# Short matmul tiles filled up with zeros to the full height: k and v in five chunks of 128 rows, the transform's row 288 in tiles of 97

## The chip, the core and the metric

One core of a Trainium2 chip runs the whole program in one launch. TensorE (PE, with its weight loads PEld) multiplies, VectorE (DVE), ScalarE (ACT) and GpSimd (POOL) work on tiles in the on-chip memory, and SyncE (SP) issues all DMA transfers of this kernel. The metric is the device time of one execution in microseconds (us), as the median of several runs; smaller is better.

## What is computed

Three layers follow each other on 8 batches, 8 heads, 576 rows and 64 channels (512 columns in all):

```python
def _attn_ref(q, k, v, g_norm):
    kv = np.einsum('bhsd,bhse->bhde', k, v)          # sums over the 576 rows
    out = np.einsum('bhsd,bhde->bhse', q, kv)
    rms = np.sqrt(np.mean(out * out, axis=-1, keepdims=True) + 1e-06)
    return out / rms * g_norm

def _moe_ref(x, w_ch1, w_ch2):
    mixed = np.real(fft(fft(x, axis=1), axis=2))     # over rows, then over columns
    u = x + mixed
    un = (u - mean(u)) / np.sqrt(var(u) + 1e-06)     # over the 512 columns
    return u + np.maximum(un @ w_ch1, 0.0) @ w_ch2   # 512 -> 2048 -> 512

def _moe2_ref(x, U, V, w_ch1, w_ch2):
    u = x + (x.T @ U @ V).T                          # over the rows, rank 32
    return u + np.maximum(u @ w_ch1, 0.0) @ w_ch2
```

## The kernel before

**Tiles and stages.** The two MLP layers run in 2 x 9 blocks of 512 rows (`BT`), each in 16 steps `n`: step `n` computes one 128-wide slice of the hidden layer (`emit_l1`, lines 168 to 170) and adds the slice before it to the outputs (`emit_l2`, lines 188 to 194). A factor is split into a high and a low part, so each product takes three matmuls with 512 moving columns.

**Attention and the transform beside the MLP.** Batch 0 goes ahead of the loop. Batches 1 to 7 are cut into pieces by `batch_tasks` and hung on fixed steps of blocks 0 to 6 through the table `side`. For batch b, `load_kv` (lines 400 to 406) brings k and v into a tile `kv` of 128 partitions: four chunks of 128 rows with two DMAs (line 404) and the last 64 rows of both with a third (line 405); for batch 0 this is done once for each half of the columns. `t_kv` (lines 237 to 249) multiplies k by v in two halves. A half has two groups of five matmuls, one for each chunk, of 128, 128, 128, 128 and 64 rows (`KT`, line 29). They are plain f32, and the trace shows each as two records of 128 columns, so a half has 20 records. `t_o` (line 262) multiplies q by the result; `t_norm` and the `t_fold_` functions prepare the transform on DVE, ACT and POOL.

**The transform over the rows.** By symmetry 289 of the 576 rows are left: 256 in two full tiles, 33 in a third. `seq_dft` (lines 336 to 347) adds up six full matmuls of 290 columns. For the cosine half (p = 0) there follows one of a single row, row 288 (line 345: `z288` from the table, `e288` from the data, both at partition 32), and then one of 97 rows that holds the remaining 32 rows three times (line 347; 96 rows for the sine half). `t_s1` calls it for two column halves and both p, `t_mu` once for the means. `e288` is made for each batch by ACT (line 321) and DVE (line 334); `z288` once, from the table `cz` (line 225). The transform over the columns is `t_s2` (lines 373 to 375).

**Order.** `manual_schedule` keeps every engine's instructions in the order in which the code issues them, and each engine's queue runs in that order. SP's queue carries all loads and stores, among them the MLP's weights in 64-bit form (`raw`, line 77, two buffers), which DVE, ACT and POOL turn into f32 (`w_conv` in block 0, `w_pre` in blocks 1 to 7). A weight load is issued when the conversion before it has read its buffer.

Of the kernel before, what the change touches and what calls it, by code (L numbers as in the profile page):

```python
# [10 lines left out]
F32 = mybir.dt.float32  # L11
F32R = mybir.dt.float32r
U32 = mybir.dt.uint32
AF = mybir.ActivationFunctionType
ALU = mybir.AluOpType
# [4 lines left out]
B, H, S, D = 8, 8, 576, 64  # L20
NH = S // 2 + 1
DM, DFF, RANK = 512, 2048, 32
# [3 lines left out]
NQ = 4 * C + 98  # L26
NS = 290
ND = 258
KT = (128, 128, 128, 128, 64)
BT = 512  # L30
NB = NT // BT
NF = DFF // 128
# [2 lines left out]


@with_exitstack
def kernel(ctx: ExitStack, tc: tile.TileContext, qT, kvm, kvt, gn, w1a, w2a, w1b, w2b,
                      ucat, v4, tabs, outT):
    nc = tc.nc  # L40
    f32 = lambda ap: ap.bitcast(F32)
# [12 lines left out]
    def side_bank(nm):  # L54
        if early:
            k = len(early) % 6
            early.append(True)
            if k < 4:
                return ps_acc.tile([128, 512], F32, tag=f"acc{k}", name=nm)
        return ps_s.tile([128, 512], F32, tag="side", name=nm)  # L60
# [7 lines left out]
    xe0 = com.tile([C, 3, B], F32, name="xe0")  # L68
# [130 lines left out]
    at = att_ctx.enter_context(tc.tile_pool(name="at", bufs=1))  # L199
# [3 lines left out]
    tb = {}  # L203
# [11 lines left out]
    def split_table(nm):  # L215

        t = tb.pop(nm)
        p, n = t.shape
        h = at.tile([p, n], F32R, name=nm + "h")
        nc.scalar.activation(out=h, in_=t, func=AF.Copy)  # L220
        if nm[1] == "z":
            nc.gpsimd.tensor_tensor(out=h[32:64], in0=t[32:64], in1=f32(h[32:64]), op=ALU.subtract)
            if nm == "cz":
                z = at.tile([33, n], F32R, name="z288")
                nc.scalar.activation(out=z[32:33], in_=t[96:97], func=AF.Copy)
                tb["z288"] = z[32:33]
            tb[nm] = h
            return
        l = at.tile([p, n], F32R, name=nm + "l")
        nc.gpsimd.tensor_tensor(out=l, in0=t, in1=f32(h), op=ALU.subtract)  # L230
        tb[nm + "h"], tb[nm + "l"] = (v.rearrange("p (k n) -> p k n", k=2) for v in (h, l))

    st = {}

    kvbd = com.tile([128, 4, 128], F32, name="kvbd")

    def t_kv(b, half):
        kv = st[b]["kv"]
        ps = side_bank(f"kv{b}_{half}")
        for j in range(2):  # L240
            cols = slice(256 * half + 128 * j, 256 * half + 128 * j + 128)
            for t in range(5):
                n = KT[t]
                nc.tensor.matmul(out=ps[:, 128 * j:128 * j + 128], lhsT=kv[:n, 0, t, cols], rhs=kv[:n, 1, t, cols],  # L244
                                 start=(t == 0), stop=(t == 4))
        pv = ps[:, 0:256].rearrange("p (j e) -> p j e", j=2)
        pairs = slice(2 * half, 2 * half + 2)
        nc.scalar.activation(out=kvbd[0:64, pairs, 0:64], in_=pv[0:64, :, 0:64], func=AF.Copy)
        nc.vector.tensor_copy(out=kvbd[64:128, pairs, 64:128], in_=pv[64:128, :, 64:128])
# [36 lines left out]
    def t_fold_s(b, c):  # L286
        s = st[b]
        if c == 0:
            s["f"] = at.tile([C, 2, 3, DM + 256], F32, tag="slot_a", name=f"f{b}")
            s["eh"] = at.tile([C, 2, 2, 2, 256], F32R, tag="slot_b", name=f"eh{b}")  # L290
            s["ez"] = at.tile([97, 2, 256], F32R, tag="ez", name=f"ez{b}")
            s["e288"] = at.tile([33, 256], F32R, tag="e288", name=f"e288_{b}")[32:33]
        m = C if c < 2 else RL
        f, x = s["f"], s["x"]
        nc.vector.tensor_tensor(out=f[:m, 0, c, 0:DM], in0=x[:m, 0, c], in1=x[:m, 1, c], op=ALU.add)
        nc.gpsimd.tensor_tensor(out=f[:m, 1, c, 0:DM], in0=x[:m, 0, c], in1=x[:m, 1, c], op=ALU.subtract)
# [7 lines left out]
    def pile(dst, src):  # L304

        nc.scalar.activation(out=dst[0:32], in_=src[0:32], func=AF.Copy)
        nc.scalar.activation(out=dst[32:64], in_=src[0:32], func=AF.Copy)
        nc.scalar.activation(out=dst[64:64 + RL], in_=src[0:RL], func=AF.Copy)

    def pile_low(dst, src):  # L310
        nc.vector.tensor_tensor(out=dst[0:32], in0=src[0:32], in1=f32(dst[0:32]), op=ALU.subtract)
# [24 lines left out]
    def seq_dft(out, p, hi, lo, z, z288):  # L336

        th, tl = (tb["csh"], tb["csl"]) if p == 0 else (tb["ssh"], tb["ssl"])
        tz = tb["cz" if p == 0 else "sz"]
        for kt in range(2):  # L340
            nc.tensor.matmul(out=out, lhsT=lo[kt], rhs=th[:, kt, :], start=(kt == 0), stop=False)
            nc.tensor.matmul(out=out, lhsT=hi[kt], rhs=tl[:, kt, :], start=False, stop=False)
            nc.tensor.matmul(out=out, lhsT=hi[kt], rhs=th[:, kt, :], start=False, stop=False)
        if p == 0:
            nc.tensor.matmul(out=out, lhsT=z288, rhs=tb["z288"], start=False, stop=False)
        m = tz.shape[0]
        nc.tensor.matmul(out=out, lhsT=z[0:m], rhs=tz, start=False, stop=True)

    def t_s1(b, p, ec):
        s = st[b]  # L350
        if p == 0 and ec == 0:
            s["y"] = at.tile([128, 2, 2, 2, NS], F32R, tag="slot_c", name=f"y{b}")
        eh = s["eh"]
        cols = slice(128 * ec, 128 * ec + 128)
        ps = side_bank(f"s1_{b}_{p}_{ec}")
        seq_dft(ps[:, :NS], p, [eh[:, p, 0, k, cols] for k in range(2)], [eh[:, p, 1, k, cols] for k in range(2)],
                s["ez"][:, p, cols], s["e288"][:, cols])
        y = s["y"]
        nc.scalar.activation(out=y[:, p, 0, ec], in_=ps[:, :NS], func=AF.Copy)
        nc.vector.tensor_tensor(out=y[:, p, 1, ec], in0=ps[:, :NS], in1=f32(y[:, p, 0, ec]), op=ALU.subtract)  # L360
# [37 lines left out]
        st.setdefault(b, {})["q"] = q  # L398

    def load_kv(b):  # L400
        kv = at.tile([128, 2, 5, DM], F32, tag="slot_a", name=f"kv{b}")
        for c in (slice(0, 256), slice(256, 512)) if b == 0 else (slice(0, 512),):
            for a in range(2):
                nc.sync.dma_start(out=kv[:, a, 0:4, c], in_=kvm[b][:, a, :, c])
            nc.sync.dma_start(out=kv[0:64, :, 4, c], in_=kvt[b][:, :, c])
        st.setdefault(b, {})["kv"] = kv

    def batch_tasks(b):
# [100 lines left out]
    mus = {}  # L509

    def t_mu(step):
        if step == 0:
            eh = at.tile([C, 2, 2, B], F32R, name="xe0s")
            ez = at.tile([97, B], F32R, name="xe0z")
            e288 = at.tile([33, B], F32R, name="xe0_288")[32:33]
            mus["e"] = eh, ez, e288
            nc.scalar.activation(out=eh[:, 0], in_=xe0[:, 0:2], func=AF.Copy)
            nc.vector.tensor_tensor(out=eh[:, 1], in0=xe0[:, 0:2], in1=f32(eh[:, 0]), op=ALU.subtract)
            pile(ez, xe0[:, 2])
            pile_low(ez, xe0[:, 2])  # L520
            nc.scalar.activation(out=e288, in_=xe0[32:33, 2], func=AF.Copy)
            nc.vector.tensor_tensor(out=e288, in0=xe0[32:33, 2], in1=f32(e288), op=ALU.subtract)
            return
        eh, ez, e288 = mus["e"]
        ps = side_bank("mu")
        seq_dft(ps[:B, :NS], 0, [eh[:, 0, k] for k in range(2)], [eh[:, 1, k] for k in range(2)], ez, e288)
        m = at.tile([B, NS], F32, name="mu_s")
        nc.vector.tensor_copy(out=m, in_=ps[:B, :NS])
        nc.sync.dma_start(out=mu_d[:, 0:289], in_=m[:, 0:289])
        nc.sync.dma_start(out=mu_d[:, 289:576], in_=m[:, 1:288])  # L530
        with nc.allow_non_contiguous_dma(reason="4608 means, once"):
            nc.sync.dma_start(out=muT, in_=mu_d.rearrange("b s -> (b s)").rearrange("(i p) -> p i", p=128))
# [143 lines left out]
    with tc.manual_schedule():  # L676
        make_identity(nc, ident)
        nc.vector.memset(nhalf, -0.5)
        nc.vector.memset(kvbd, 0.0)
        nc.vector.memset(ebias, -896.0 * 2.0 ** 23)  # L680
        load_kv(0)
        load_q(0)
        nc.sync.dma_start(out=gnb, in_=gn)
# [15 lines left out]
        for c in range(3):  # L699
            for k in range(2 * c, min(2 * c + 2, 5)):  # L700
                t_norm(0, k)
            if c:
                t_fold_h(0, c - 1, 0)
            t_fold_s(0, c)
            t_fold_e(0, c, 0)
            for nm in (("cs", "cz"), ("ss", "sz"), ("cd",))[c]:
                split_table(nm)
# [71 lines left out]
        for n in range(2 * NA):  # L779
            i, j = n % NF, n // NF  # L780
# [107 lines left out]
```

## Time and profile before

| | |
|---|---|
| median of 3 runs | 1957.66 us (1957.63 to 1962.66) |
| profiled execution | 1957.75 us, of which the trace's span is 1956.0 us |
| busy share of the span | PE 95%, PEld 78%, DVE 51%, ACT 40%, POOL 39% |
| mean DMA rate | 72 GB/s |

The span falls into four stages:

| stage, us | what runs | length | PE busy | DVE busy | granted clock |
|---|---|---|---|---|---|
| 0 to 79.4 | batch 0 and k, v of batch 1 | 79.4 | 37.48 | 52.70 | 0.74 |
| 79.4 to 235.6 | block 0, batch 1 beside it | 156.2 | 122.77 | 132.64 | 0.88 |
| 235.6 to 937.5 | blocks 1 to 6 and the start of block 7, batches 2 to 7, the means | 701.9 | 674.68 | 470.24 | 0.99 |
| 937.5 to 1956 | the rest | 1018.5 | 1014.63 | 345.25 | 1.00 |

How to read it: a matmul's record lasts longer than the distance to the next record, because matmuls overlap. So what a matmul costs is read here as the step from its start to the next start. The granted clock is the mean share of TensorE's full 2.4 GHz; its two levels are 1.2 and 2.4 GHz.

### The profile page before, as it was taken

The numbers are of one execution on the slowest core, as the hardware profiler recorded it, in microseconds if no ns is written. First come the engines' busy times: TensorE is split into PE (matmuls) and PEld (weight loads), VectorE is DVE, ScalarE is ACT, GpSimd is POOL, SyncE is SP. The second block draws the span as 40 slices with busy tenths as digits, with TensorE's granted clock in tenths as the row PEclk, the third lists the DMA queues.
The fourth block names the chain that finished last, engine by engine and source line by source line (L and its number), as shares of the span: only waits on it lengthen the run. The fifth ranks groups of instructions, "written<-read, shape, count | busy, mean of one in ns | idle before, by whom it ended". The sixth has DMA issues, their size and how long they took to land.

```text
span 1956.0 us, 22839 instructions
## 1 busy us (share of the span) xinstructions
PE 1849.6 (95%) x8520; PEld 1516.8 (78%) x8520; DVE 1000.8 (51%) x1525; ACT 780.0 (40%) x1460; POOL 769.8 (39%) x592
## 2 busy tenths in 40 slices
PE   4667899999899998999999999999999999999999
PEld 3556678878787887878888888888888888888887
DVE  5898785776757576574443333333333333333232
ACT  4444344444434444343434343434343433333332
POOL 4486665554545554453322223232223222222322
PEclk7878999999999999999999999999999999999999
DMA  4524415133241422302303301010101010100000
GB/s 137 192 86 150 174 44 193 68 119 130 73 146 54 163 98 97 133 10 74 87 33 131 122 1 49 1 44 1 49 0 44 1 49 1 44 1 22 1 22 22
DMA packets 62545, 140.05 MB, mean 72 GB/s; under 512 B 11273, under 2 KB 13786, under 8 KB 59618
## 3 DMA queue, kind: packets, MB, share of 16 engines
q1 hardware_dynamic: 62434, 138.59, 20.7%
q8 instruction: 67, 1.10, 0.2%
q14 instruction: 44, 0.36, 0.1%
HBM read 100.78 MB, written 36.73 MB: 70 GB/s over the span
## 4 chain that ended last, share of the span: by engine, by line
PE 75%; DVE 12%; POOL 6%; issue 3%; DMA 2%; ACT 2%; SPq 0%; DVEq 0%; POOLq 0%; ACTq 0%
PE h L168 11%; PE h L170 11%; PE h L169 11%; PE acc L193 7%; PE acc L194 7%; PE acc L192 7%; PE acc L188 4%; PE acc L190 4%; PE acc L189 4%; POOL ss L269 2%; PE kv L244 2%; POOL x L282 2%; DMA raw<-in_w2a 2%; DVE f L301 2%; DVE eh L330 1%
## 5 line engine op out<-in xcount | busy, mean ns | idle before, releaser
L146 POOL TENSOR_TENSOR w1l<-w,w1h 128x512 fp32r<-128x512 f32 x274 | 357.3, 1304 | 976.6 <-ACT w1h L145 953.3
L174 DVE SCALAR_TENSOR_TENSOR gl<-h,gh 128x512 fp32r<-128x512 f32 x288 | 198.3, 689 | 393.5 <-ACT gh L173 393.4
L173 ACT ACTIVATE gh<-h 128x512 fp32r<-128x512 f32 x288 | 171.4, 595 | 502.8 <-PE h L170 502.7
L154 DVE TENSOR_TENSOR w2l<-w,w2h 128x512 fp32r<-128x512 f32 x283 | 208.9, 738 | 188.4 <-ACT w2h L153 187.6
L188 PE MATMUL acc<-w2h,gl 128*128 128x512 f32 x576 | 235.4, 409 | 46.0 <-DVE gl L174 45.9
L153 ACT ACTIVATE w2h<-w 128x512 fp32r<-128x512 f32 x288 | 180.8, 628 | 160.7 <-PE acc L194 113.0
L189 PE MATMUL acc<-w2l,gh 128*128 128x512 f32 x576 | 232.0, 403 | 7.3 <-POOL w2l L154 7.3
L168 PE MATMUL h<-xl,w1h 128*128 128x512 f32 x576 | 230.0, 399 | 2.9 <-ACT w1h L145 1.4
L190 PE MATMUL acc<-w2h,gh 128*128 128x512 f32 x576 | 231.6, 402 | 0.0
L168 PE MATMUL h<-xlb,w1h 128*128 128x512 f32 x576 | 231.1, 401 | 0.0
L170 PE MATMUL h<-xhb,w1l 128*128 128x512 f32 x576 | 228.3, 396 | 0.0
L170 PE MATMUL h<-xh,w1l 128*128 128x512 f32 x576 | 226.2, 393 | 2.2 <-POOL w1l L146 2.2
L169 PE MATMUL h<-xhb,w1h 128*128 128x512 f32 x576 | 228.1, 396 | 0.0
L169 PE MATMUL h<-xh,w1h 128*128 128x512 f32 x576 | 226.2, 393 | 0.0
L194 PE MATMUL acc<-gh,w2h 128*128 128x512 f32 x576 | 225.4, 391 | 0.0
L193 PE MATMUL acc<-gl,w2h 128*128 128x512 f32 x576 | 225.4, 391 | 0.0
L192 PE MATMUL acc<-gh,w2l 128*128 128x512 f32 x576 | 224.7, 390 | 0.0
L145 ACT ACTIVATE w1h<-w 128x512 fp32r<-128x512 f32 x288 | 179.3, 623 | 23.2 <-POOL w L97 23.2
L188 PEld LDWEIGHTS acc<-w2h,gl 128*128 128x128 f32 x576 | 111.5, 194 | 79.2 <-DVE gl L174 56.0
L189 PEld LDWEIGHTS acc<-w2l,gh 128*128 128x128 f32 x576 | 112.2, 195 | 31.3 <-POOL w2l L154 8.7
L190 PEld LDWEIGHTS acc<-w2h,gh 128*128 128x128 f32 x576 | 112.5, 195 | 24.5
L170 PEld LDWEIGHTS h<-xh,w1l 128*128 128x128 f32 x576 | 109.3, 190 | 26.3 <-POOL w1l L146 2.6
(164 smaller groups left out, 2845.4 us busy)
## 6 DMA issues: line engine op xcount, KB each, us to landing
kv<-in_kvm SPq DMA_DIRECT2D x14, 1024.0 KB, 6.5
q<-in_qT SPq DMA_DIRECT2D x8, 1220.0 KB
x_d<-x2o SPq DMA_DIRECT2D x36, 256.0 KB, 2.1
x2f<-x_d SPq DMA_DIRECT2D x36, 256.0 KB, 3.8
outT<-o SPq DMA_DIRECT2D x36, 256.0 KB, 2.0
raw<-in_w1a SPq DMA_DIRECT2D x16, 512.0 KB, 3.4
raw<-in_w2a SPq DMA_DIRECT2D x16, 512.0 KB, 3.7
u_d<-x SPq DMA_DIRECT2D x32, 256.0 KB, 2.6
```

The source lines that it names most:

```text
L146: (nc.vector if n in on_dve else nc.gpsimd).tensor_tensor(out=al, in0=a, in1=f32(ah), op=ALU.subtract)
L154: (nc.gpsimd if n in CLP else nc.vector).tensor_tensor(out=cl, in0=c, in1=f32(ch), op=ALU.subtract)
L168: nc.tensor.matmul(out=h, lhsT=ah[:, kc, :], rhs=xl[:, kc, :], start=(kc == 0), stop=False)
L169: nc.tensor.matmul(out=h, lhsT=ah[:, kc, :], rhs=xh[:, kc, :], start=False, stop=False)
L170: nc.tensor.matmul(out=h, lhsT=al[:, kc, :], rhs=xh[:, kc, :], start=False, stop=(kc == 3))
L174: nc.vector.scalar_tensor_tensor(out=gl, in0=h, scalar=0.0, in1=f32(gh), op0=ALU.max, op1=ALU.subtract)
L188: nc.tensor.matmul(out=a, lhsT=gl[:, tt], rhs=ch, start=s, stop=False)
L189: nc.tensor.matmul(out=a, lhsT=gh[:, tt], rhs=cl, start=False, stop=False)
L190: nc.tensor.matmul(out=a, lhsT=gh[:, tt], rhs=ch, start=False, stop=e)
L192: nc.tensor.matmul(out=a, lhsT=cl[:, tt], rhs=gh, start=s, stop=False)
L193: nc.tensor.matmul(out=a, lhsT=ch[:, tt], rhs=gl, start=False, stop=False)
L194: nc.tensor.matmul(out=a, lhsT=ch[:, tt], rhs=gh, start=False, stop=e)
```

## The change

k and v come from the host as one array with 64 rows of zeros behind the 576, five chunks of 128 rows, and are loaded with two DMAs in place of three. All matmuls of `t_kv` then have 128 rows. Row 288 becomes a matmul of 97 rows in which all rows but number 32 are zero: `z288` is written whole (once, one more ACT instruction), and `e288` is one tile for the whole program, zeroed once at the start (one DVE and one ACT instruction); per batch its row 32 is written as before. `t_mu` uses the same tile. The number of matmuls and their columns do not change.

```diff
-KT = (128, 128, 128, 128, 64)
+KC = 5
...
-                z = at.tile([33, n], F32R, name="z288")
+                z = tb["z288"] = at.tile([97, n], F32R, name="z288")
+                nc.scalar.activation(out=z, in_=t, func=AF.Copy, scale=0.0)
                 nc.scalar.activation(out=z[32:33], in_=t[96:97], func=AF.Copy)
-                tb["z288"] = z[32:33]
...
+    e288 = at.tile([97, 256], F32R, name="e288")
...
-            for t in range(5):
-                n = KT[t]
-                nc.tensor.matmul(out=ps[:, 128 * j:128 * j + 128], lhsT=kv[:n, 0, t, cols], rhs=kv[:n, 1, t, cols],
-                                 start=(t == 0), stop=(t == 4))
+            for t in range(KC):
+                nc.tensor.matmul(out=ps[:, 128 * j:128 * j + 128], lhsT=kv[:, 0, t, cols], rhs=kv[:, 1, t, cols],
+                                 start=(t == 0), stop=(t == KC - 1))
...
-            s["e288"] = at.tile([33, 256], F32R, tag="e288", name=f"e288_{b}")[32:33]
+            s["e288"] = e288[32:33]
...
-                s["ez"][:, p, cols], s["e288"][:, cols])
+                s["ez"][:, p, cols], e288[:, cols])
...
-        kv = at.tile([128, 2, 5, DM], F32, tag="slot_a", name=f"kv{b}")
+        kv = at.tile([128, 2, KC, DM], F32, tag="slot_a", name=f"kv{b}")
         for c in (slice(0, 256), slice(256, 512)) if b == 0 else (slice(0, 512),):
             for a in range(2):
-                nc.sync.dma_start(out=kv[:, a, 0:4, c], in_=kvm[b][:, a, :, c])
-            nc.sync.dma_start(out=kv[0:64, :, 4, c], in_=kvt[b][:, :, c])
+                nc.sync.dma_start(out=kv[:, a, :, c], in_=kvm[b][:, a, :, c])
...
-            e288 = at.tile([33, B], F32R, name="xe0_288")[32:33]
...
+            z = e288[32:33, 0:B]
+            nc.scalar.activation(out=z, in_=xe0[32:33, 2], func=AF.Copy)
+            nc.vector.tensor_tensor(out=z, in0=xe0[32:33, 2], in1=f32(z), op=ALU.subtract)
...
+        nc.vector.memset(f32(e288), 0.0)
+        nc.scalar.activation(out=e288, in_=f32(e288), func=AF.Copy)
...
-    kvm = np.ascontiguousarray(kv[:, :, :512].reshape(B, 2, 4, 128, DM).transpose(0, 3, 1, 2, 4))
-    kvt = np.ascontiguousarray(kv[:, :, 512:].transpose(0, 2, 1, 3))
+    kvm = np.zeros((B, 2, KC, 128, DM), kv.dtype)
+    kvm.reshape(B, 2, KC * 128, DM)[:, :, :S] = kv
+    kvm = np.ascontiguousarray(kvm.transpose(0, 3, 1, 2, 4))
```

PE's order is the same in both kernels. SP's queue in block 0, where k and v of batch 2 (`kv2`) are loaded between two pairs of weight loads (`raw`), was:

```order
L77 DMA raw_1110<-in_w1a 128x1024
L77 DMA raw_1112<-in_w2a 128x1024
L404 DMA kv2_1158<-in_kvm 128x2048 x2
L405 DMA kv2_1158<-in_kvt 64x2x512
L77 DMA raw_1180<-in_w1a 128x1024
L77 DMA raw_1182<-in_w2a 128x1024
```

and is now:

```order
L77 DMA raw_1109<-in_w1a 128x1024
L77 DMA raw_1111<-in_w2a 128x1024
L404 DMA kv2_1157<-in_kvm 128x2560 x2
L77 DMA raw_1178<-in_w1a 128x1024
L77 DMA raw_1180<-in_w2a 128x1024
```

The third load is gone, and the two that are left bring 2560 in place of 2048 elements to each of 128 partitions; what follows them is the same. ACT's queue in the stage of batch 0, where the tables are split between two runs of eight norm instructions (line 278), was:

```order
L278 ACTIVATE x0_198<-x0_198,ss0_200 128x64 x8
L220 ACTIVATE csh_269<-raw_xh_164 128x580
L220 ACTIVATE czh_273<-raw_xh_164 97x290
L225 ACTIVATE z288_276<-raw_xh_164 1x290
L278 ACTIVATE x0_198<-x0_198,ss0_200 128x64 x8
```

and is now:

```order
L278 ACTIVATE x0_199<-x0_199,ss0_201 128x64 x8
L220 ACTIVATE csh_269<-raw_xh_165 128x580
L220 ACTIVATE czh_273<-raw_xh_165 97x290
L225 ACTIVATE z288_276<-raw_xh_165 97x290
L226 ACTIVATE z288_276<-raw_xh_165 1x290
L278 ACTIVATE x0_199<-x0_199,ss0_201 128x64 x8
```

One instruction of 97 rows has come in ahead of the second run; the rest stands where it stood.

## Rows read from the trace of the kernel before

**Rows 1.** The page, part 1: busy time, share, instructions.

```profile
PE 1849.6 (95%) x8520; PEld 1516.8 (78%) x8520; DVE 1000.8 (51%) x1525; ACT 780.0 (40%) x1460; POOL 769.8 (39%) x592
```

**Rows 2.** Chain of waits, blocks 1 and 2: start us, length us, engine, line.

```profile
360.19 0.61 ACT gh L173
...
405.39 0.61 DVE gl L174
...
438.61 2.81 PE kv L244 x20
```

**Rows 3.** Stretches: us, busy of PE PEld DVE ACT POOL, clock, DMA.

```profile
290.90:360.10 69.20, 69.14 (x352) 58.00 (x352) 41.34 (x71) 26.97 (x52) 30.22 (x27) 1.00 0.44 154
...
521.00:590.00 69.00, 68.93 (x344) 57.75 (x345) 41.38 (x71) 26.97 (x52) 30.21 (x27) 0.98 0.44 151
```

**Rows 4.** Timeline, PE, one `t_kv`: start us, length us, instruction, tiles.

```profile
323.44 0.27 PE L244 MATMUL kv<-kv 128*128 128x128 f32 x1
...
324.21 0.28 PE L244 MATMUL kv<-kv 128*128 128x128 f32 x1
324.42 0.37 PE L244 MATMUL kv<-kv 64*128 64x128 f32 x1
324.63 0.27 PE L244 MATMUL kv<-kv 64*128 64x128 f32 x1
324.83 0.38 PE L244 MATMUL kv<-kv 128*128 128x128 f32 x1
325.05 0.39 PE L244 MATMUL kv<-kv 128*128 128x128 f32 x2
```

**Rows 5.** Timeline, PE and then PEld, one `seq_dft` with row 288.

```profile
294.52 0.29 PE L343 MATMUL s<-csh,eh 128*128 128x290 f32 x1
294.75 0.40 PE L345 MATMUL s<-z,e 1*128 1x290 f32 x1
295.07 0.40 PE L347 MATMUL s<-czh,ez 97*128 97x290 f32 x1
295.31 0.30 PE L341 MATMUL s<-csh,eh 128*128 128x290 f32 x1
295.45 0.30 PE L342 MATMUL s<-csl,eh 128*128 128x290 f32 x1
...
294.75 0.18 PEld L345 LDWEIGHTS s<-z,e 1*128 1x128 f32 x1 [0.17 <-issue]
```

**Rows 6.** Timeline, PE, the end of `t_mu`.

```profile
936.93 0.29 PE L345 MATMUL mu<-z,xe 1*8 1x290 f32 x1
937.15 0.30 PE L347 MATMUL mu<-czh,xe0z 97*8 97x290 f32 x1
937.29 0.40 PE L168 MATMUL h<-xl,w1h 128*128 128x512 f32 x1
```

**Rows 7.** Chain of waits, the first 16 us.

```profile
1.25 5.21 DMA kv<-in_kvm
...
6.60 9.24 PE kv L244 x40
```

**Rows 8.** Timeline, PE, batch 0's `seq_dft`.

```profile
42.44 0.44 PE L342 MATMUL s<-csl,eh 128*128 128x290 f32 x1
42.68 0.44 PE L343 MATMUL s<-csh,eh 128*128 128x290 f32 x1
...
44.05 0.44 PE L341 MATMUL s<-csh,eh 128*128 128x290 f32 x1
```

**Rows 9.** Timeline, ACT, batch 0; in brackets the idle time ahead, and its releaser.

```profile
25.12 0.44 ACT L225 ACTIVATE z<-raw_xh 1x290 fp32r<-1x290 f32 x1
...
36.87 0.63 ACT L284 ACTIVATE x<-x 34x512 f32<-34x512 f32 x1 [7.96 <-DVE x L282]
```

**Rows 10.** Block 0: DVE's timeline, then a stretch as in rows 3.

```profile
179.57 0.43 DVE L85 TENSOR_SCALAR cv<-raw 128x512 uint32<-128x512 uint32 x1 [3.37 <-DMA raw<-in_w1a]
...
172.00:174.00 2.00, 1.95 (x11) 1.44 (x11) 0.92 (x2) 0.96 (x3) 2.00 (x2) 1.00 1.01 399
```

More of the change, by code (lines that the diff above doesn't have):

```diff
@@ L37, with kernel @@
 @with_exitstack
-def kernel(ctx: ExitStack, tc: tile.TileContext, qT, kvm, kvt, gn, w1a, w2a, w1b, w2b,
+def kernel(ctx: ExitStack, tc: tile.TileContext, qT, kvm, gn, w1a, w2a, w1b, w2b,
                       ucat, v4, tabs, outT):
@@ L514, in t_mu @@
             ez = at.tile([97, B], F32R, name="xe0z")
-            e288 = at.tile([33, B], F32R, name="xe0_288")[32:33]
-            mus["e"] = eh, ez, e288
+            mus["e"] = eh, ez
             nc.scalar.activation(out=eh[:, 0], in_=xe0[:, 0:2], func=AF.Copy)
@@ L520, in t_mu @@
             pile_low(ez, xe0[:, 2])
-            nc.scalar.activation(out=e288, in_=xe0[32:33, 2], func=AF.Copy)
-            nc.vector.tensor_tensor(out=e288, in0=xe0[32:33, 2], in1=f32(e288), op=ALU.subtract)
+            z = e288[32:33, 0:B]
+            nc.scalar.activation(out=z, in_=xe0[32:33, 2], func=AF.Copy)
+            nc.vector.tensor_tensor(out=z, in0=xe0[32:33, 2], in1=f32(z), op=ALU.subtract)
             return
-        eh, ez, e288 = mus["e"]
+        eh, ez = mus["e"]
         ps = side_bank("mu")
-        seq_dft(ps[:B, :NS], 0, [eh[:, 0, k] for k in range(2)], [eh[:, 1, k] for k in range(2)], ez, e288)
+        seq_dft(ps[:B, :NS], 0, [eh[:, 0, k] for k in range(2)], [eh[:, 1, k] for k in range(2)], ez, e288[:, 0:B])
         m = at.tile([B, NS], F32, name="mu_s")
@@ L869 @@
     arrays = {
-        "qT": qT, "kvm": kvm, "kvt": kvt, "gn": g,
+        "qT": qT, "kvm": kvm, "gn": g,
         "w1a": w1(inputs["moe_w_ch1"]), "w2a": w2(inputs["moe_w_ch2"]),
@@ L880 @@
     with tile.TileContext(nc) as tc:
-        kernel(tc, *(aps[n] for n in ("qT", "kvm", "kvt", "gn", "w1a", "w2a", "w1b", "w2b", "ucat", "v4")),
+        kernel(tc, *(aps[n] for n in ("qT", "kvm", "gn", "w1a", "w2a", "w1b", "w2b", "ucat", "v4")),
                           tabs, out)
```

## The prediction, made before the changed kernel was run

> **What bounds the kernel now.** I read the page's busy shares first: PE is busy for 95% of the span, no other engine for more than 51% [rows 1]. The table of stages then says where the missing time lies: PE stands still in the first 235 us, while from 235.6 to 937.5 us it is busy for 674.68 of 701.9 us, and after that always. So a change to PE is worth its full price only where the chain of waits runs on PE, and the chain is what I read next. In each of the blocks 1 to 6 it looks the same: soon after the block's start it leaves PE for ACT, at 360.19 us in block 2, goes through the attention work of DVE, POOL and ACT, and comes back to PE with DVE's `gl` at 405.39, just ahead of the next matmul at 406 [rows 2]. From there it stays on PE until the next block. Both things that the change touches stand in the PE part: `seq_dft` runs some 4 us after the chain's return, `t_kv` another 30 and 40 us later (438.61 in block 2 [rows 2]). In such a part nothing else is near its limit: from 290.9 to 360.1 us PE is busy for 69.14 of 69.20 us, DVE for 41.34, POOL for 30.22 [rows 3].
>
> **What a short tile costs.** I read it from the steps between starts. In `t_kv` the first eight records, all of 128 rows, have started by 324.21; seven steps took 324.21 - 323.44 = 0.77 us, 0.11 us each. Then come the 64 rows' two records and two of full height, at 324.42, 324.63, 324.83 and 325.05: four steps of some 0.21 us, 0.84 us in place of 0.44 [rows 4]. The excess is 0.40 us by these rounded rows; I take 0.39. It is no matter of rows multiplied: the records between full ones take 0.11 us, and the second record of 64 rows, which follows one of its own height, is as late as the first. What is missing is the overlap with the weight load: a full tile's weights are loaded while the matmul before it runs, but PEld stood idle for 0.17 us ahead of the single row's weights and started them with the matmul itself, at 294.75 [rows 5]. Around row 288 the starts are 294.52, 294.75, 295.07, 295.31: three steps, 0.79 us in place of 3 x 0.135 (the next step is 295.45 - 295.31 = 0.14) [rows 5], so again 0.39 us: each site has one way into the short height and one way out.
>
> Whether 97 rows count as full height decides half of the change. `t_mu` shows it, since its weights have only 8 columns and are loaded in no time: the single row starts at 936.93, the 97 rows at 937.15 (0.22 us, a change of height), the full tile of `emit_l1` at 937.29, 0.14 us later, a plain step [rows 6]. So 97 rows beside 128 cost nothing, and I cost the new matmuls of row 288 like their neighbours.
>
> A rule of the Trainium skill speaks against the change: "TensorE: Matmul & The Clock Gate", Part 3, says that a weight load overlaps a running matmul only when its row group differs, which would make the short tile the one whose weights hide. By that rule of the Trainium skill the change would give nothing on PE (rival 2), where the rows give 0.39 us a site; here the trace disagrees.
>
> **The sum, part by part.**
>
> *Blocks 1 to 7, from 235.6 us.* `t_kv` runs for batches 3 to 7, two halves with two 64-row chunks each: 5 x 4 = 20 chunks at 0.39 = 7.8 us. Behind each of the five first halves comes a matmul of `t_s2` with only 34 columns of weights, whose exposed load is shorter by about three quarters of its 0.1 us: -0.4, so 7.4 us. Row 288 comes twice for each of batches 2 to 7: 12 x 0.39 = 4.7 us. `t_mu`: the steps 0.22 and 0.22 lose about 0.09 each, 0.2 us. All of it lies on the chain: **12.3 us**. In this stage nothing else on the path changes. Each load of k and v grows from 2.36 to 2.62 MB, but it is issued five steps `n` before it is used; DVE and ACT do per batch what they did.
>
> *Batch 0, up to 79.4 us.* PE begins when two loads of 0.52 MB each have landed, 5.21 us after the issue [rows 7]; each now has 0.66 MB. The extra 0.26 MB cost between 0.26 / 0.399 = 0.7 us (the rate of a large load [rows 10]) and a quarter of 5.21, 1.3 us (the rate of these loads): I take 0.9. The 64 rows used to come in a third load that eight matmuls covered. Against that the stretch of 40 records, 9.24 us [rows 7], loses four short chunks, and runs partly at the lower clock, where row 288 costs more: 42.68 to 44.05 us is 1.37 for three steps of 0.24 [rows 8], 0.65 us too long. Four chunks give 4 x 0.39 to 4 x 0.65, that is 1.6 to 2.6; I take 2.0. The net is between +0.3 and +1.9; as the later start may leave more matmuls at the lower clock, I widen it to -0.4 to +1.9 and take **0.5 us**. The two row-288 sites of batch 0 stand on the chain at the lower clock: 1.3 us at most; as the clock rises shortly after, and some of the matmuls behind it come forward into the slow time, **1.0 us** (0.7 to 1.3). ACT's new instruction, 0.44 us by its one-row sister [rows 9], is hidden: ACT later idles 7.96 us until DVE is done [rows 9], and DVE uses the second run of norms last. If that cover were gone it would cost its 0.44. The zeroing of `e288` falls into the time before the first load lands.
>
> *Block 0, 79.4 to 235.6 us.* DVE is busy for 132.64 of 156.2 us and the chain runs over weight loads and conversions. Here stand row 288 of batch 1 (2 sites) and `t_kv` of batch 2 (4 chunks), 2.3 us of PE's time, which PE spends waiting instead: I take 0 (0 to 2.3). And here SP issues two weight loads behind the load of k and v; DVE waited 3.37 us for the first of them [rows 10]. That load moved 399 GB/s [rows 10], and 0.26 MB more keep the weights back by 0.65 us, which nothing hides: **-0.65 us** (0 to -1.3). `t_kv` and `load_kv` have no new wait, and fewer DMAs stand in SP's queue.
>
> The sum is 12.3 + 0.5 + 1.0 - 0.65 = 13.15 us. From the profiled execution's 1957.75 us, of which 1.75 lie outside the span, this gives 1944.6; the median of the runs shown is only 0.1 us lower, so **1944.6 us**.
>
> **What the clock may add or take.** Of the six PE parts (blocks 1 to 6 and the start of block 7) five show a granted clock of 1.00, like the first of rows 3; from 521 to 590 us, behind a wait of PE, it was 0.98 [rows 3]: 0.02 x 69 = 1.4 us for a stretch at the lower level. Every block has such waits, and which of them the clock answers may change when the work before them moves by a few us. I allow for one such stretch less and two more: +1.4 to -2.8 us.
>
> So the forecast's own range is from 12.3 + 1.9 + 1.3 + 1.4 = 17 (1941) to 12.3 - 0.4 + 0.7 - 1.3 - 2.8 = 8.5 us gained (1949).
>
> **The rivals.**
>
> 1. *Given back between the blocks.* If the attention work in a block's first 45 us doesn't start earlier when PE does, PE waits longer instead. Then only what comes behind the last such wait counts, row 288 of batch 7 and `t_mu`, 1.0 us, and batch 0's 1.5, less 0.65: about 1956. For it speaks that DVE and POOL carry those 45 us; against it that the chain goes into them from PE's own matmuls [rows 2] and that DVE has 28 of 69 us free before [rows 3]. 0.07.
> 2. *The short height is not the cause.* If the weights of the filled tiles don't hide either, PE gains nothing and the extra bytes cost 0.65 in block 0 and 0.9 at the start: 1959.3. The hidden loads of all other full tiles speak against it [rows 4 to 6]. 0.03.
> 3. *The change does only half*: a tile of 97 rows with row 32 alone filled still counts as another height. Then 4.7, 0.2 and 1.0 us are missing: 1950.5. The 97 rows in `t_mu` [rows 6] speak against it. 0.05.
> 4. *Block 0 passes the gain on*, all 2.3 us, batch 0 gives its upper ends (1.9 + 1.3, 1.7 more than taken), and there is one low stretch less: 13.15 + 2.3 + 1.7 + 1.4 = 18.6, 1939.2. DVE's share in block 0 speaks against it. 0.05.
> 5. *Slower: the clock.* The waits ahead of the PE parts stay; each could be answered by a stretch at the lower level, for 1.4 us. One of six PE parts has one now. From ten more of them the change is slower than before, and with fourteen, more than two for each part, it stands at 13.15 - 19.6 = 6.5 us lost, 1964. It would have to strike nearly every wait of these blocks, of which most were answered by nothing. 0.02.
>
> **Chances and range.** The forecast has 0.78. About 0.3% (5.9 us) is what a measurement of this kernel can tell from no change. Faster by more: the forecast, rivals 3 and 4, 0.88. Within: rivals 1 and 2, 0.10. Slower: 0.02. The range reaches over the forecast's own and over rival 3, 1940.5 to 1951; left out are rivals 1, 2, 4 and 5, 0.17.
>
> **What would show it.** In the profile after, all 20 records of a `t_kv` half should step by 0.11 us, 2.2 us for the half in place of 2.2 + 2 x 0.39 = 3.0; the steps at row 288 should be 0.13; PE's busy time should fall by 15 us or more, since its work in block 0 shrinks too; the wait of DVE in rows 10 should be 0.6 us longer; and the stage from 235.6 to 937.5 us should be 12 us shorter. I am wrong if that stage keeps its length while the steps shrink (rival 1), if the steps stay at 0.21 (rival 2), or if the clock column of rows 3 falls below 0.98 in most blocks (rival 5).

## The result and the profile after

| | before | after |
|---|---|---|
| median of 4 runs on one chip | 1959.74 us (1957.63 to 1962.66) | 1942.37 us (1941.54 to 1944.11) |
| profiled execution, span in brackets | 1957.75 us (1956.0) | 1941.54 us (1939.7) |

The ratio is 0.9914, 95% interval 0.9898 to 0.9929: 17.4 us less by the medians, 16.3 us by the two traces. Measured again beside other kernels, the changed one took 1941.51 us (1940.75 to 1942.39, 4 runs) beside 1961.02 (1953.39 to 1965.38, 23 runs) of the one before: 0.9896 [0.9883, 0.9909]. Forecast were 1944.6, in a range of 1940.5 to 1951. The kernel before scatters by more than the changed one, and its profiled execution is one of its faster ones; so the two traces compared below show a smaller gain than the medians do.

The first part of the page, as [rows 1]: PE has lost 21.0 us of busy time with the same number of instructions, DVE, ACT and POOL at most 0.8.

```profile
PE 1828.6 (94%) x8520; PEld 1509.4 (78%) x8520; DVE 1000.8 (52%) x1526; ACT 779.9 (40%) x1462; POOL 769.0 (40%) x592
```

The view by stretches for the four stages, then for three of the PE parts and for 3.4 us of the second of these (columns as in [rows 3]):

```profile
0.00:76.70 76.70, 32.05 (x203) 30.14 (x203) 53.12 (x92) 31.22 (x76) 34.21 (x33) 0.73 0.55 189
76.70:231.00 154.30, 118.90 (x515) 94.23 (x515) 132.68 (x196) 75.00 (x140) 112.81 (x74) 0.89 0.41 142
231.00:921.00 690.00, 662.80 (x3312) 558.20 (x3313) 469.92 (x731) 296.28 (x592) 349.72 (x275) 0.99 0.29 103
921.00:1939.70 1018.70, 1014.83 (x4494) 826.80 (x4492) 345.06 (x509) 377.40 (x654) 272.23 (x212) 1.00 0.10 34
...
286.10:353.30 67.20, 67.00 (x352) 57.36 (x352) 41.50 (x71) 26.91 (x52) 30.08 (x27) 1.00 0.46 162
398.00:464.97 66.97, 65.75 (x339) 56.28 (x340) 41.82 (x72) 27.79 (x54) 30.43 (x27) 0.97 0.43 154
512.00:577.80 65.80, 64.09 (x338) 54.98 (x339) 41.86 (x71) 28.21 (x55) 30.45 (x27) 1.00 0.45 157
...
400.70:404.10 3.40, 3.40 (x11) 2.82 (x10) 2.22 (x5) 2.68 (x6) 0.58 (x1) 0.50 0.38 78
```

Batch 0's stage is 2.7 us shorter (76.7 for 79.4), block 0 by 1.9 (154.3 for 156.2), blocks 1 to 7 by 11.9 at these rounded edges (690.0 for 701.9; 11.6 from matmul to matmul), the rest by nothing. The block 1 part that takes the place of the first of [rows 3] is 67.20 us in place of 69.20, with the same 352 matmuls. The low clock has moved: it stood in block 3, from 521 us on [rows 3], and now stands in block 2, 400.7 to 404.1 us, at 0.50, the 1.2 GHz level.

The timeline of PE, the counterparts of [rows 4 to 6]: a half of `t_kv` and the matmul behind it, row 288 with its neighbours, and the end of `t_mu`; then PEld at row 288.

```profile
317.97 2.39 PE L244 MATMUL kv<-kv 128*128 128x128 f32 x20
320.12 0.36 PE L373 MATMUL s<-cdh,y 128*34 128x258 f32 x1
...
289.86 0.30 PE L343 MATMUL s<-csh,eh 128*128 128x290 f32 x1
290.00 0.29 PE L345 MATMUL s<-z,e 97*128 97x290 f32 x1
290.13 0.30 PE L347 MATMUL s<-czh,ez 97*128 97x290 f32 x1
290.26 0.30 PE L341 MATMUL s<-csh,eh 128*128 128x290 f32 x1
...
920.75 0.30 PE L345 MATMUL mu<-z,e 97*8 97x290 f32 x1
920.88 0.30 PE L347 MATMUL mu<-czh,xe0z 97*8 97x290 f32 x1
921.02 0.40 PE L168 MATMUL h<-xl,w1h 128*128 128x512 f32 x1
...
290.00 0.19 PEld L347 LDWEIGHTS s<-czh,ez 97*128 97x128 f32 x1
```

The half takes 320.12 - 317.97 = 2.15 us for 20 records. Row 288 stands in a row of steps of 0.13 or 0.14, and the weights of the matmul behind it are loaded at 290.00, while it runs itself; the weights of the single row were loaded only when their own matmul began [rows 5].

The chain of waits, from block 2 (as [rows 2]):

```profile
353.39 0.61 ACT gh L173
...
398.56 0.61 DVE gl L174
...
400.93 0.43 PE acc L188
401.36 0.43 PE acc L189
...
432.61 2.23 PE kv L244 x20
```

The chain still leaves PE for ACT and comes back with DVE's `gl`, both 6.8 us earlier than in [rows 2]: between them nothing is gained and nothing is given back. `t_kv` is only 6.0 us earlier. Of the 6.8, two sites of row 288 in between added 0.8, and the stretch at the lower clock, with steps of 0.43 for 0.23, took back 1.6.

### The profile page after: what moved, and what is told of

Same layout as the page of the kernel before. It is cut to its first block, busy times and chain, and to the rows that moved or that the text cites. A ratio compares the mean times of both kernels' runs of the same rounds, so it can differ in the third digit from the quotient of the medians.

```text
span 1939.7 us, 22822 instructions
## 1 busy us (share of the span) xinstructions
PE 1828.6 (94%) x8520; PEld 1509.4 (78%) x8520; DVE 1000.8 (52%) x1526; ACT 779.9 (40%) x1462; POOL 769.0 (40%) x592
## 4 chain that ended last, share of the span: by engine, by line
PE 74%; DVE 13%; POOL 6%; issue 3%; ACT 3%; DMA 2%; SPq 0%; DVEq 0%; POOLq 0%; ACTq 0%
PE h L168 11%; PE h L170 11%; PE h L169 11%; PE acc L193 7%; PE acc L194 7%; PE acc L192 7%; PE acc L188 4%; PE acc L190 4%; PE acc L189 4%; POOL ss L269 2%; POOL x L282 2%; DVE f L301 2%; PE kv L244 2%; DVE eh L330 1%; DMA raw<-in_w2a 1%
```

## The experiments

**The two parts, each by itself.** First k and v as in the changed kernel, with row 288 as before.

```diff
-KT = (128, 128, 128, 128, 64)
+KT = (128, 128, 128, 128, 128)
...
-                nc.sync.dma_start(out=kv[:, a, 0:4, c], in_=kvm[b][:, a, :, c])
-            nc.sync.dma_start(out=kv[0:64, :, 4, c], in_=kvt[b][:, :, c])
+                nc.sync.dma_start(out=kv[:, a, :, c], in_=kvm[b][:, a, :, c])
...
```

> k and v alone are changed (two loads of five chunks, all t_kv matmuls of 128 rows); row 288 as in the kernel before. Theory H (a change of tile height costs PE 0.19 us, and each 64-row chunk has two): a t_kv half takes 2.15 us in place of 2.90, the steps at row 288 stay 0.22, 0.32, 0.24; blocks 1 to 7 gain 7.4 us. The start of block 0 comes about 2 us earlier, since TensorE's first 40 records lose their height changes. Theory L (the two larger loads, not PE, shorten block 0): DVE's wait for the weight load behind k and v of batch 2 is about 1.7 us as in the changed kernel, and block 0 gains about 2 us here too. Together a span of about 1945. If H is wrong and the gain came from row 288, the span stays above 1950.

1949.0 us (1946.18 to 1949.49), 0.9933 [0.9909, 0.9956]. Then row 288 alone:

```diff
-                z = at.tile([33, n], F32R, name="z288")
+                z = tb["z288"] = at.tile([97, n], F32R, name="z288")
...
+    e288 = at.tile([97, 256], F32R, name="e288")
...
-                s["ez"][:, p, cols], s["e288"][:, cols])
+                s["ez"][:, p, cols], e288[:, cols])
...
```

> Row 288 alone is changed (97 rows with zeros), k and v as in the kernel before. Theory H: steps at row 288 of 0.13 us, 4.7 + 0.2 us gained in blocks 1 to 7, t_kv halves stay at 2.90 us. Theory L: block 0 keeps DVE's wait of about 3.4 us for the weight load and gains nothing; batch 0 gains at most 0.5 us, as DVE and ACT set its pace there. Span about 1950.5. Rival (row 288 gains in block 0 as well, 2 us): 1948.5 or less, with the wait of DVE shorter.

1952.9 us (1950.74 to 1957.54), 0.996 [0.9947, 0.9973]. Each part shortens its own steps and leaves the other's (0.22, 0.33, 0.23 at row 288 in the first, 2.90 us for a half in the second). By the medians that is 12.8 and 8.9 us less than the kernel before, together 21.7, beside 20.2 for both (the third-load kernel below, measured at the same time); by the spans of the traces 9.2 and 4.6, together 13.8, beside 16.5. So they add up within 3 us, no closer.

**The loads alone**: five chunks in two DMAs, but matmuls of 64 rows on the last.

```diff
-                nc.sync.dma_start(out=kv[:, a, 0:4, c], in_=kvm[b][:, a, :, c])
-            nc.sync.dma_start(out=kv[0:64, :, 4, c], in_=kvt[b][:, :, c])
+                nc.sync.dma_start(out=kv[:, a, :, c], in_=kvm[b][:, a, :, c])
...
```

> Only the loads are changed (two of five chunks in place of three); the fifth chunk is multiplied with its 64 rows as before, row 288 too. Theory H: all PE steps as in the kernel before, blocks 1 to 7 gain nothing. Theory L: DVE's wait for the weight load in block 0 falls from 3.4 to about 1.7 us and block 0 gains 1.5 to 2 us; PE's first matmul starts about 0.5 us later, as in the changed kernel, and batch 0 gains nothing. Span 1954 to 1956. Rival (the larger loads only carry more bytes and cost 0.65 us in block 0): 1956.5 to 1957.5.

1959.68 us (1955.19 to 1963.27), 0.9992 [0.9977, 1.0006]. So the time comes from the matmuls. But by the traces this kernel lost 3.0 us in batch 0, where all 40 records of `t_kv` came slowly (see *Batch 0* below), and gained 1.7 us in block 0. The next two runs ask why block 0 gained.

**The third load, full height**: the changed kernel, with the fifth chunk in a load of its own into all 128 partitions.

```diff
-                nc.sync.dma_start(out=kv[:, a, :, c], in_=kvm[b][:, a, :, c])
+                nc.sync.dma_start(out=kv[:, a, 0:4, c], in_=kvm[b][:, a, :, c])
+            nc.sync.dma_start(out=kv[:, :, 4, c], in_=kvt[b][:, :, c])
...
```

> The changed kernel, but with the fifth chunk (128 rows with the zeros) in a third load of its own, rows of 2 KB, as in the kernel before. All of PE's work is that of the changed kernel and so are the bytes. Theory L (the third load with its short rows holds the weight loads up): DVE's wait in block 0 is back at 3.4 us or more, and the span is 1.5 to 3 us above the changed kernel's 1939.7. Rival (the bytes alone count, or block 0 gained through PE): wait and span as in the changed kernel.

1941.59 us (1940.7 to 1943.85), 0.99 [0.9881, 0.9919]. A third load with rows of 2 KB costs nothing that can be told here.

**The same chunk in two loads into 64 partitions each:**

```diff
+            for r in (slice(0, 64), slice(64, 128)):
+                nc.sync.dma_start(out=kv[r, :, 4, c], in_=kvt[b][r, :, c])
...
```

> The changed kernel with the fifth chunk (64 rows and 64 rows of zeros) brought by two loads of 64 partitions each; bytes and PE's work are the same as in the changed kernel and in e4_third_load, where one load of 128 partitions did it. Theory W (a load into 64 partitions alone moves at about half the rate): in block 0 the first weight load behind k and v of batch 2 lands about 13 us after the load of k and v was issued, where the kernel before had 12.7, e4_third_load 11.3 and the changed kernel 11.0; block 0 loses 1.5 to 2 us against e4_third_load, span 1941 to 1942. Rival (it was the order of block 0's other work, not the load): 11.3 us and no loss.

1944.24 us (1942.79 to 1946.85), 0.9922 [0.991, 0.9935]. Four timelines show the load of batch 2's k and v, as SP's queue issues it, and DVE's first conversion of the weights that stand behind it: before (its conversion is in [rows 10]), after, third load at full height, two loads of 64.

```profile
166.78 0.81 SPq L404 DMA_DIRECT2D kv<-in_kvm  x2
```

```profile
164.00 0.80 SPq L404 DMA_DIRECT2D kv<-in_kvm  x2
175.10 0.43 DVE L85 TENSOR_SCALAR cv<-raw 128x512 uint32<-128x512 uint32 x1 [1.67 <-DMA raw<-in_w1a]
```

```profile
162.78 0.80 SPq L404 DMA_DIRECT2D kv<-in_kvm  x2
174.10 0.43 DVE L85 TENSOR_SCALAR cv<-raw 128x512 uint32<-128x512 uint32 x1 [1.89 <-DMA raw<-in_w1a]
```

```profile
164.47 0.81 SPq L404 DMA_DIRECT2D kv<-in_kvm  x2
178.11 0.43 DVE L85 TENSOR_SCALAR cv<-raw 128x512 uint32<-128x512 uint32 x1 [4.21 <-DMA raw<-in_w1a]
```

From the issue to the conversion: 179.57 - 166.78 = 12.8 us before, 11.1 after, 11.3 with the third load of full height, 13.6 with two loads of 64, though the last three move the same bytes and the first 0.26 MB less. The other kernels fall in line: 12.4 us for the two that load as before, 11.1 to 11.6 for all that load 128 partitions. The view by stretches says where (last column GB/s): before, after, third load at full height, two loads of 64.

```profile
174.00:176.00 2.00, 2.00 (x14) 1.86 (x13) 0.72 (x2) 0.83 (x2) 1.33 (x2) 1.00 1.04 236
```

```profile
170.00:172.00 2.00, 1.69 (x12) 1.69 (x13) 0.62 (x2) 0.48 (x2) 2.00 (x3) 1.00 0.95 401
172.00:174.00 2.00, 2.00 (x12) 1.69 (x11) 0.92 (x2) 0.41 (x1) 0.51 (x1) 1.00 1.01 412
```

```profile
170.00:172.00 2.00, 2.00 (x14) 1.87 (x13) 0.70 (x2) 0.82 (x2) 1.31 (x2) 1.00 1.04 416
```

```profile
172.00:174.00 2.00, 2.00 (x13) 1.78 (x13) 0.92 (x2) 0.83 (x2) 1.00 (x1) 1.00 1.03 201
174.00:176.00 2.00, 2.00 (x10) 1.65 (x9) 0.00 (x0) 0.00 (x0) 0.00 (x0) 1.00 1.04 255
```

While a load into 64 partitions is under way the rate falls from some 400 to between 201 and 255 GB/s, though the DMA engines stay busy (1.03, 1.04); with full height it stays at 401 to 416. So the 64 partitions are the cause of the late weights, not a third load, its short rows or its bytes.

**What a change of height costs.** Before, with the short chunks of a half side by side: the number of short matmuls stays, the changes of height are halved.

```diff
-            for t in range(5):
+            ts = (0, 1, 2, 3, 4) if j == 0 else (4, 0, 1, 2, 3)
+            for t in ts:
...
-                                 start=(t == 0), stop=(t == 4))
+                                 start=(t == ts[0]), stop=(t == ts[-1]))
```

> The kernel before with one change of order: in each t_kv half the second group begins with its 64-row chunk, so that the two short chunks of a half stand beside each other. As many short matmuls with as many rows as before, half as many changes of height. Theory H (the change of height costs, not the short matmul): a half takes 2.15 + 0.39 + a little for the loads between the two short chunks (they can't hide before one another if short tiles never hide theirs: up to 0.2) = 2.5 to 2.75 us in place of 2.90, 1.5 to 4 us over blocks 1 to 7. Rival (each short matmul costs by itself): 2.90 as before and no gain.

The timeline of PE, one half (the second row is the four records of 64 rows, the third the first two of full height behind them):

```profile
325.25 2.78 PE L245 MATMUL kv<-kv 128*128 128x128 f32 x20
...
326.24 0.71 PE L245 MATMUL kv<-kv 64*128 64x128 f32 x4
...
326.88 0.49 PE L245 MATMUL kv<-kv 128*128 128x128 f32 x2
...
327.79 0.36 PE L374 MATMUL s<-cdh,y 128*34 128x258 f32 x1
```

The half takes 2.54 us, between 2.90 with four changes and 2.15 with none. The last three of the short records step by 0.21, 0.11 and 0.11 us, so short tiles hide their loads behind each other too; only the first two records behind each change come late, by about 0.1 each. The price belongs to the change and is 0.19 us with weights of 128 columns. The whole kernel, 1960.69 us (1955.4 to 1962.78), 0.999 [0.9979, 1.0], gained in its undisturbed blocks 0.6 of the 0.78 us that two sites give; against its scatter of 7 us in ten runs that is too little to show.

**Row 288 in a tile of 33 rows**, from partition 0: is it the height or the start at partition 32?

```diff
-            nc.tensor.matmul(out=out, lhsT=z288, rhs=tb["z288"], start=False, stop=False)
+            nc.tensor.matmul(out=out, lhsT=z288[0:33], rhs=tb["z288"][0:33], start=False, stop=False)
```

> The changed kernel, but the matmul of row 288 uses the first 33 rows of its zero-filled tiles in place of 97, so it starts at partition 0 and is still a tile of less than 65 rows. Theory H (the height of the tile decides): two changes of height at each site again, steps of 0.22, 0.32, 0.24 us, 0.39 a site, 12 sites in blocks 1 to 7 on the chain: the span is about 4.7 us above that of the changed kernel (1939.7 and 1940.5 in its two profiles), so 1944 to 1946. Rival P (the single row was slow because its tile began at partition 32): steps of 0.13 us and the span of the changed kernel.

```profile
291.85 0.29 PE L343 MATMUL s<-csh,eh 128*128 128x290 f32 x1
292.07 0.40 PE L345 MATMUL s<-z,e 33*128 33x290 f32 x1
292.40 0.41 PE L347 MATMUL s<-czh,ez 97*128 97x290 f32 x1
292.64 0.30 PE L341 MATMUL s<-csh,eh 128*128 128x290 f32 x1
```

The steps in this timeline of PE are 0.22, 0.33 and 0.24 us, as with the single row [rows 5]: 1949.22 us (1948.11 to 1951.59), 0.9948 [0.9935, 0.9961]. So 33 rows that start at partition 0 are as short as one row at partition 32, and 97 are full; heights between 64 and 96 were not run.

**The same cure at a place the change left alone.** `t_pt` (line 597) has eight pairs of matmuls of 64 rows, one for each batch, in the last stage, where PE never stops. They get 128 rows, of which the added ones meet rows of zeros in the factor; ACT and DVE prepare 128 rows for them too.

```diff
+        r0, r1 = 0, 128
...
-        r0, r1 = pt_rows(b, k)
+        r0, r1 = 0, 128
```

> The changed kernel, and the last short tiles that are left are filled up too: in t_pt of the second layer, the eight sites where only 64 of a tile's 128 rows belong to the batch multiply all 128, the other rows by the zeros that the table u1 already holds there. Theory H: at such a site the changed kernel's steps are 0.32, 0.34, 0.32, 0.34 us where 0.23 is plain; all four fall to 0.23, 0.4 us a site, 8 sites, on a stretch in which PE never waits: 3.2 us less than the changed kernel run beside it, and half a wait less anywhere else. Rival (PE's time follows the rows that are multiplied): the same time or a little more, as 64 rows become 128. DVE and ACT work on 128 rows at these sites, which takes no longer by their rows (0.69 and 0.63 us).

The timeline of PE at one site, in the changed kernel and here:

```profile
1049.80 0.39 PE L190 MATMUL acc<-w2h,gh 128*128 128x512 f32 x1
1050.12 0.73 PE L597 MATMUL pt<-x2s,u 64*128 64x512 f32 x2
1050.78 0.50 PE L168 MATMUL h<-xl,w1h 128*128 128x512 f32 x1
```

```profile
1049.10 0.40 PE L190 MATMUL acc<-w2h,gh 128*128 128x512 f32 x1
1049.33 0.62 PE L598 MATMUL pt<-x2s,u 128*128 128x512 f32 x2
1049.79 0.39 PE L168 MATMUL h<-xl,w1h 128*128 128x512 f32 x1
```

The pair comes 0.32 in place of 0.23 us after its neighbour and takes 0.66 in place of 0.46, and the matmul behind it is late by another 0.1. The last stage is 3.0 us shorter, 0.38 a site: the same price with 512 moving columns as with 128 or 290. At 1938.25 us (1937.67 to 1939.76), 0.9882 [0.9866, 0.9897], beside 1941.51 of the changed kernel on the same chip, this is the fastest version.

**Scatter.** The changed kernel was measured again, unchanged:

> The changed kernel itself, run beside e7_pt_full and e8_b0_full for comparison. Its runs should lie close together, within some 4 us, where those of the kernel before lie 10 us apart, if the scatter of the kernel before comes from its first t_kv (theory C, below in e8_b0_full); rival: the same scatter.

1941.51 us, 0.9896 [0.9883, 0.9909]. Its four runs lie 1.6 us apart, 2.6 the first time, those of the kernel before 5 in four runs and 12 in 23. Two kernels ask where that comes from. First the loads alone, with batch 0's `t_kv` at full height too:

```diff
-                n = KT[t]
+                n = 128 if b == 0 else KT[t]
```

> As e3_loads_only (the loads of the changed kernel, all else as before), but batch 0's t_kv multiplies the fifth chunk with all 128 rows; batches 1 to 7 and row 288 stay short. Theory C: without the height changes in PE's very first stretch the clock rises within it (step 0.21 to 0.11 us) after some 4.5 us of matmuls, as in the changed kernel and e1_kv_only, so the 40 records take some 6.8 us, and block 0 begins 4 to 5 us earlier than in e3_loads_only, whose clock stayed low for all 10.9 us; the time lies 3 to 5 us below that of e3_loads_only and the runs scatter less than its 8 us. Rival (when the clock rises is chance, whatever the tiles' height): the 40 records take between 8 and 11 us in one profile or another, and time and scatter are those of e3_loads_only, less 1.6 us for the eight height changes.

1957.55 us, 0.998 [0.9968, 0.9992], with eleven runs between 1952.96 and 1961.76; a twelfth took 10377.7 us, for which no trace gives a reason, and is left out here. Then the changed kernel with five unread matmuls of full height more in each half of `t_kv` for batches 2 to 7, which give back most of the length without a change of height:

```diff
+        if b > 1:
+            for t in range(KC):
+                nc.tensor.matmul(out=ps[:, 256:384], lhsT=kv[:, 0, t, 0:128], rhs=kv[:, 1, t, 0:128],
...
```

> The changed kernel with work added back: each t_kv half of batches 2 to 7 multiplies one column group of 128 once more, five plain matmuls of full height (10 records of 0.11 us) into a part of the bank that nobody reads. That is 2.2 us more for each block, as much as the change had taken away, but without a change of height. Theory S (the scatter of the kernel before, 10 us against 3 of the changed kernel, comes from how a block's length meets the clock's changes, not from the short tiles): the runs scatter over 7 us or more again. Rival: they lie within 4 us as those of the changed kernel. Time by either: 5 blocks x 2.2 = 11 us above the changed kernel, about 1952.5, block 0 taking its share for nothing.

1956.47 us (1953.62 to 1959.4), 0.9985 [0.9976, 0.9994]. The view by stretches, two of its PE parts:

```profile
634.50:637.90 3.40, 3.40 (x11) 2.73 (x10) 2.32 (x5) 2.78 (x6) 0.48 (x1) 0.50 0.39 87
750.50:753.90 3.40, 3.40 (x9) 2.66 (x9) 2.56 (x6) 2.80 (x6) 0.23 (x1) 0.50 0.30 55
```

Five plain matmuls are ten records and took 1.04 us by their timeline. Ten such halves in blocks 1 to 5 are 10.4 us, and the two stretches at 0.50, against one in the changed kernel, 1.5 more: 11.9 us, where those blocks and what follows are 12.2 longer. Block 0, with two halves, is 2.0 longer. This accounts for the 13.9 us between the traces.

Set against the kernel before, the blocks of all traces can be read this way. Gain in us from the start of one block to the next, a star where a PE part of that block has a stretch with a granted clock of 0.50; since the kernel before has its own in block 3, a block 3 without a star is better by 1.5:

| kernel | block 1 | 2 | 3 | 4 | 5 | 6 |
|---|---|---|---|---|---|---|
| after | 2.1 | 0.5* | 3.7 | 2.2 | 2.1 | 0.8 |
| after, second trace | 2.2 | 2.2 | 3.8 | 2.2 | 2.2 | -0.7* |
| k and v alone | 1.5 | 1.4 | 2.9 | -0.1* | 1.4 | -1.5* |
| row 288 alone | 0.9 | 0.8 | 2.4 | -0.7* | -0.8* | -0.8* |
| loads alone | 0.1 | 0.1 | 0.0* | -1.5* | 0.1 | 0.1 |
| `t_pt` full as well | 2.2 | 2.1 | 3.6 | 2.2 | 2.1 | 0.8 |
| with filler | 0.0 | 0.0 | 1.6 | -1.5* | -1.7* | 0.9 |

Every entry is the price of its steps (2.2, 1.45, 0.8 or 0) and, for a star, 1.5 to 1.7 less. The traces of the five kernels that are not shown read the same way, but for block 2 of the two loads of 64, which has no star and gave 1.7 in place of 2.2. The stars also go some way to explain why several spans came out 1 to 3 us above what was expected: the kernel with 33 rows (1947.7 us) has three, k and v alone and the two loads of 64 have two each. The stretch in block 2 of after begins 1.5 us after PE's first matmul behind a wait (399.2 us), the first of the filler's 1.4; others, such as one at 499.7 us after, fall into the part that runs on DVE and cost nothing. Such stretches, 1.5 us each, could make up much of the scatter, but there is one trace for each kernel (two for the changed one), and batch 0's start differs from run to run as well: no run settles why the kernels with 64-row tiles in `t_kv` scatter most. Batch 0's tiles are not it alone (9 us without them). The filler, which has no short tiles in `t_kv` or at row 288, scattered by 6 us in 12 runs, between the 4 and the 7 us of the two theories, so it decides for neither; and a range grows with the number of runs, of which the changed kernel had only four at a time.

## Why the prediction was right, point by point

*Blocks 1 to 7, 12.3 us:* right in size and in its reasons. Measured, from matmul to matmul, 11.6 and, in the second trace, 12.1. An undisturbed block gave 2.1 to 2.2 us where the sum had 1.48 for `t_kv` and 0.78 for row 288; `t_mu` gave its 0.2. One reading in it was wrong without harm: the weights of 8 columns in `t_mu` are not loaded in no time, their records on PEld take 0.08 us (0.19 for 128 columns).

*97 rows count as full:* right. Rival 3 falls with the 0.13 steps. Rival 2 falls too, and with it the rule of the Trainium skill that the prediction had set against the rows: PEld loads full tiles while the matmul before runs.

*Batch 0, 1.5 us in all:* measured 2.7, so it was sized too small, and part of the surplus is chance. The first k by v came 0.5 us later (forecast 0.9), the stretch of 40 records fell by 2.4 (forecast 2.0). Chains of waits of after, of its second trace, and of the loads alone, as [rows 7]:

```profile
1.24 5.70 DMA kv<-in_kvm
7.07 6.86 PE kv L244 x40
```

```profile
2.97 10.62 DMA q<-in_qT
13.73 1.14 PE o L262 x8
```

```profile
6.77 10.73 PE kv L244 x39
```

That stretch took 6.2 to 10.9 us in the kernels above, 7.7 in one whose `t_kv` is as before (row 288 alone). Its steps begin at 0.21 us, twice the plain 0.11, and halve at a moment that differs from run to run: 7.0 us after the first matmul before, 4.5 after, 3.7 with row 288 alone, between 3 and 15 in all traces. The clock's column reads 1.00 up to there only because there is no entry behind it: in every trace the list of clock intervals begins just where the steps halve, at 13.6 us before, 11.6 after, 10.1 in its second trace and 21.9 with the loads alone. So the prediction's lower clock fits the steps, though no entry shows it. As an estimate, 2.5 us less at the doubled step (7.0 less 4.5) make 1.2 of the 2.4 us; with row 288 alone the steps halved as early although its `t_kv` has the 64-row tiles, so this part can't be put down to the change.

The floor was not in the sum: `t_o` waits for `q`, which lands at 13.5 to 14.6 us in the nine traces that show it, however early the products are done. From the first matmul of row 288's sums to block 0 the kernels with the tile of 97 rows gained 0.3 to 1.9 us, those without -0.5 to 0.8: the 1.0 of the sum lies inside, and the run hides it. ACT's new instruction was hidden, as forecast: after it ACT still idles 7.56 us ahead of line 284.

*Block 0, -0.65 us:* wrong in sign, and this is the step that failed. It priced 0.26 MB at 399 GB/s [rows 10] and bounded the delay at nothing, so that a gain was left out, although the change also takes away a load into 64 partitions, whose rate the next row of the same view would have shown (236 GB/s). DVE's wait for the weights fell from 3.37 to 1.67 us where 0.6 more was forecast. Block 0 gained 1.9 us, 0.6 in the second trace and 1.7 with the loads alone; over all nine traces whose loads reach 128 partitions (the filler among them) it lay between -0.4 and 1.9, 0.9 in the mean, while the two other kernels with three loads as before lost 0.5 and 0.6 and the one with two loads of 64 lost 1.2. So the earlier landing is shown in every trace; what it is worth in block 0, some 1 us, only as the mean of groups that nearly touch. PE's own share, taken as 0, can't be told apart from that spread.

*The clock, +1.4 to -2.8:* one stretch in a PE part before and one after, so nothing on balance, and 1.5 us a stretch as priced. Rivals 1 and 5 didn't come: the chain's return in block 2 was as much earlier as its departure, and no stage's clock fell by more than 0.01 (batch 0, 0.73 for 0.74). Rival 4 came near in size, 1.65 us net in block 0 for 1.9 measured, but not in its cause, since the loads alone did as much without a shorter step.

*The total:* 11.6 + 2.7 + 1.9 = 16.2 for 13.15, where 2.6 of the 3.1 us too little are block 0's. The profiled execution took 1941.54 us, 3.1 less than forecast. The forecast came true by its main term, which was 0.7 too large; batch 0 and block 0 gave 1.2 and 2.6 more than priced, and the sum of these errors stayed inside the range. The medians give a larger gain, 17.4 and 19.5 us; what these sums leave out of it is the scatter of the kernel before, which no run explains.

## What to carry to other kernels

Look for lone short matmul tiles, of 64 rows or fewer, between full ones: each such site (of 1, 33 and 64 rows) cost 0.39 us here at the full clock, with 128, 290 or 512 moving columns and weights of 128 columns, and zeros up to 97 or 128 rows cost nothing on TensorE; where zeros can't be had, put the short ones side by side. Count a load by the partitions that it reaches, not by its bytes alone. Price such a gain only where the chain of waits runs on PE.

## What the runs showed of the hardware that was not expected

- While a load into 64 partitions was under way the rate was 201 to 255 GB/s, with one into 128 some 400; with one load for each half it stayed low through both. The Trainium skill, "SBUF — State Buffer", section "Door 1: The DMA port swizzle", says that a transfer's bandwidth depends on how many of 16 ports its partitions reach; by its table 64 adjoining ones reach half of them. The trace agrees, and the prediction would have had the sign from it.
- Behind each change of height two records come late, not one, also the second of the new height. In `t_mu` before, where the weights have 8 columns, only the first does: steps of 0.22 and 0.22, then a plain 0.14 [rows 6], so that site cost 0.2 us and not 0.39. About half of the price thus goes with the columns of the weights; why the other half is there, the traces don't say. The Trainium skill, "TensorEngine Tiling (Array Packing)", section "Key Properties", says that a change of tiling mode drains TensorE; the 0.19 us would fit that, but no run shows the array drained.
- Four runs of the kernel before lay 5 us apart, four of the changed one 1.6 and 2.6; why is open.
